# The MLP's gate row in four column tiles, sent through DRAM to all partitions, and the doubled columns of the norms on VectorE

## The chip, the cores and the metric

The kernel runs on one core of a Trainium2 chip. The metric is the device time of one execution in microseconds; the median of several runs is compared. A core has TensorE (PE; its weight loads are shown apart as PEld), VectorE (DVE), ScalarE (ACT), GpSimd (POOL) and SyncE (SP), which run side by side and wait for one another through semaphores. SyncE and GpSimd also issue most of the DMAs: SyncE's go to the queue that the profile calls q1, GpSimd's to q0. An engine takes its instructions in the order of the program, so an instruction that waits holds up everything behind it on that engine, DMA issues included.

## The reference

A transformer block on x of 2048 x 576, with a conditioning vector c. `mod` is a row of six vectors of 576: shift, scale and gate for the attention (sa, ca, ga) and for the MLP (sb, cb, gb).

```python
mod = (silu(c) @ w_mod).reshape(c.shape[0], 6, 1, -1)
sa, ca, ga, sb, cb, gb = ...
h = layernorm(x) * (1 + ca) + sa
x = x + ga * A(h, wqkv, wo)          # 32 heads of 18, each position sees 8 positions, 2 apart
h = layernorm(x) * (1 + cb) + sb
x = x + gb * (((h @ w_gate) * (h @ w_up)) @ w_down)     # 576 -> 4608 -> 576
return x
```

The change touches how gb is computed and spread, and one part of how layernorm's output is written.

## The kernel before

The 2048 rows are cut into eight chunks of 256, each of two tiles of 128 rows. The chunks form five groups for the MLP: [0], [1, 2], [3, 4], [5, 6], [7]. A setup stage (to about 48 us) computes the modulation, the whole attention of chunk 0 and parts of chunks 1 and 2. Then, for every group, `gate_up` computes gate, up and their product hh over 36 steps f of 128 hidden columns, and `down` multiplies hh with w_down. Between the steps of one group stand pieces of the attention of the next chunks, so that TensorE always has matmuls.

The order on every engine is that of the program text. The function `timed` decides it: it walks over the gate steps of a group, keeps a clock of TensorE (`t`) and one of VectorE, and places a waiting piece as soon as the marks that it needs are due. A piece is a tuple (TensorE time, VectorE time, needed marks, its mark, time until the mark, call). The numbers are estimates written by hand; a different estimate for one piece can move other pieces to another step. A gate step is a pair of half matmuls: `Pair.first` of the new step stands ahead of `Pair.second` of the one before.

D is 576, P is 128. 576 columns are four full tiles of 128 and a rest of 64, so the last tile of weights has only 64 rows. For the matmuls of pairs, which use the array as two halves of 64 rows, the last 64 columns of the normalized rows are written twice (columns 512 to 575 and again 576 to 639): the "doubled columns". `norm` (L280) does both writes on VectorE, `norm_act` (L287) does both on ScalarE, after a small VectorE instruction for the bias (L285). `norm_act` writes the doubled columns for chunk 3 ahead of the attention and for chunk 1 ahead of the MLP.

`mod_row` computes one row of 576 of the modulation already spread over all 128 partitions: `sc_bc` holds silu(c) in 128 equal columns, so each output partition gets the same row. That is two PSUM tiles (512 and 64 columns) with five matmuls each (L356) and two copies on ScalarE (L358, L359). It is used for ga (in the setup) and for gb: `gb_row`, which is a piece of group 0's `gate_up`. gb_bc, 128 x 576 in f32, is read for the first time at the end of group 0's `down`, where VectorE multiplies acc and accr with it (L949, L954, in the last group L996).

The weights of the gate row are loaded by `load_wm5` on GpSimd's queue: four row tiles into the free end of the hh tile, the last 64 rows into an output tile (wm5r, shown as o_t). Behind it on the same queue stand `load_wd(0)` and then, in `gb_row` after `mod_row`, `ld_d1(3)`: the load of block 3 of w_down, 576 KB, also into the free end of hh.

Weights of gate and up come in nine blocks per group (four steps each), gate and up as one load of 512 KB each, on SyncE's queue (L154). In group 0, blocks 0 to 2 are loaded in the setup, block 3 goes to the free end of hh, block 4 is asked for at step 4, block 5 at step 8, and so on. Step f uses block f // 4. On the same queue stand the transposes by DMA: of the normalized rows of chunk 3 into hT (L394), and of the attention's logits into lg_t (L487). The kernel starts its projections of chunk 3 (`qk_pair`, L706 with wqk) when hT has been modulated by VectorE (L302).

PSUM tiles are taken in turn from eight banks. Each DMA queue counts its DMAs on eight semaphores in turn, so that an issue also waits for the DMA eight places earlier.

Of the kernel before, what the change touches and what calls it, by code (L numbers as in the profile page):

```python
# [7 lines left out]
BF = mybir.dt.bfloat16  # L8
F32 = mybir.dt.float32
ALU = mybir.AluOpType  # L10
ACTF = mybir.ActivationFunctionType
# [7 lines left out]
P = 128  # L19
D = 576  # L20
DP = 640
KT = 5
KF = 4
H = 32
# [2 lines left out]
DIL = 2  # L27
FF = 4608
FT = FF // P
HALO = 16  # L30
SPAN = 14
EPS = 1e-5
# [12 lines left out]
def kernel(  # L45
# [13 lines left out]
    nc = tc.nc  # L59
# [9 lines left out]
    consts = pool("consts", 1)  # L69
    wts = pool("wts", 1)  # L70
    dramp = pool("dramp", 1, space=DRAM)
# [19 lines left out]
    def ps(shape, dt, name):  # L91
        return psp.tile(shape, dt, name=name, tag="bank")
# [8 lines left out]
    eps = consts.tile([P, 1], F32, name="eps")  # L101
    modc = consts.tile([P, 4, KT], F32, name="modc")
    ga_bc = consts.tile([P, D], F32, name="ga_bc")
    gb_bc = consts.tile([P, D], F32, name="gb_bc")
    sc_bc = consts.tile([P, KT, P], BF, name="sc_bc")
    xns = [consts.tile([P, ST, DP], BF, name=f"xn{k}") for k in range(2)]
    o_sb = consts.tile([P, ST, DP], BF, name="o_sb")
# [2 lines left out]
    qTs = [consts.tile([P, KT, CH], BF, name=f"qT{k}") for k in range(2)]  # L110
    kTs = [consts.tile([P, KT, HALO + CH], BF, name=f"kT{k}") for k in range(2)]
    oT = consts.tile([P, KT, CH], BF, name="oT")
    wv = wts.tile([P, KT, D], BF, name="wv")
    wo = wts.tile([P, KT, D], BF, name="wo")
    vd = dramp.tile([HALO + S, D], BF, name="vd")
    prod_t = consts.tile([P, 4 * KT * CH], BF, name="prod_t")
    prod_n = [0]

# [19 lines left out]
    def load_res(i):  # L138
        x_res[i] = xres.tile([P, ST, D], BF, name="x_r")
        nc.sync.dma_start(x_res[i][:], x_rows(i))  # L140

    wgu_blk, wgu_in, wd_blk, wd_home, wgu_home = {}, {}, {}, {}, {}
    NG = len(GROUPS)
    NBLK = FT // FB

# [17 lines left out]
    def load_wd(g):  # L163
        if g >= NG * NBLK:
            return
        r0 = (g % NBLK) * FB * P
        wb = wd_home.pop(g, None)
        if wb is None:
            wb = wdp.tile([P, FB, D], BF, name="wd")
        wd_blk[g] = wb  # L170
        return nc.gpsimd.dma_start(wb[:], B_w_down[r0:r0 + FB * P, :].rearrange("(k p) n -> p k n", p=P))  # L171
# [38 lines left out]
    for xn_t in xns:  # L210
# [12 lines left out]
                            pattern=[[-1, P + 2 * SPAN]], channel_multiplier=1)  # L223
    zrow = sp.tile([HALO, D], BF, name="zrow")
    nc.gpsimd.memset(zrow[:], 0.0)
    nc.gpsimd.dma_start(vd[0:HALO, :], zrow[:])
    nc.gpsimd.memset(wqk[64:, KF, :], 0.0)
    for k in range(2):
# [10 lines left out]
                            base=-DIL * (W - 1), pattern=[[DIL, W], [0, H]], channel_multiplier=1)  # L239
    edge = sp.tile([HALO, W - 1, P], BF, name="edge")  # L240
    edge_t = sp.tile([P, HALO], BF, name="edge_t")
    ash_e = sp.tile([P, H], BF, name="ash_e")
# [17 lines left out]
    def ln_parts(src, tag, act=False, both=None):  # L260
        stats = small.tile([P, ST, 2, 6], F32, name="ln_stats" + tag)
        mv = small.tile([P, ST, 2], F32, name="ln_mv" + tag)
        rstd = small.tile([P, ST], F32, name="ln_rstd" + tag)
        xn = xns[turn[0] % 2]
        turn[0] += 1
        both = tag == "b" if both is None else both

        def stat(j, hfs=(0, 1)):
            for hf in hfs:
                nc.vector.bn_stats(stats[:, j, hf, :], src(j)[:, hf * 288:(hf + 1) * 288])  # L270
            if hfs[-1] == 1:
                nc.vector.bn_aggr(mv[:, j, :], stats[:, j, :, :].rearrange("p a b -> p (a b)"))

        def rsq(r):
            nc.scalar.activation(rstd[:, r], mv[:, r, 1], ACTF.Ln, bias=eps[:])
            nc.scalar.activation(rstd[:, r], rstd[:, r], ACTF.Exp, scale=-0.5)

        def norm(j):
            for d0, s0, n in ((0, 0, D), (D, D - 64, 64))[0:2 if both else 1]:
                nc.vector.tensor_scalar(xn[:, j, d0:d0 + n], src(j)[:, s0:s0 + n], mv[:, j, 0:1], rstd[:, j:j + 1],  # L280
                                        ALU.subtract, ALU.mult)

        def norm_act(j):
            nb = small.tile([P, 1], F32, name="ln_nb")
            nc.vector.scalar_tensor_tensor(nb[:], mv[:, j, 0:1], -1.0, rstd[:, j:j + 1], ALU.mult, ALU.mult)  # L285
            for d0, s0, n in ((0, 0, D), (D, D - 64, 64))[0:2 if both else 1]:
                nc.scalar.activation(xn[:, j, d0:d0 + n], src(j)[:, s0:s0 + n], ACTF.Identity, bias=nb[:], scale=rstd[:, j:j + 1])  # L287
        return xn, stat, rsq, (norm, norm_act) if act is None else norm if not act else norm_act

    def layernorm(src, tag, act=False, both=None):  # L290
# [30 lines left out]
    def mod_columns(wm, pi, fill=lambda: None, steps={}):  # L321
        pm = ps([P, 320], F32, "pm")
        order = (KF, 0, 1, 2, 3)
        for kt in order:
            for q in range(4):
                rows = slice(0, P) if kt < KF else slice(64 * (q // 2), 64 * (q // 2) + 64)
                c0 = (q // 2) * D + (q % 2) * 256
                nc.tensor.matmul(pm[H * q:H * (q + 1), :], lhsT=sc_bc[rows, kt, 0:H], rhs=wm[rows, kt, c0:c0 + 320],
                                 start=(kt == order[0]), stop=(kt == order[-1]), skip_group_check=True)
            steps.get(kt, nop)()  # L330
        mrow = sp.tile([P, 320], BF, name="mrow")
        nc.scalar.copy(mrow[:], pm[:])
        fill()
        tr = ps([P, 3, P], BF, "pm_t")
        for n in range(2):
            nc.tensor.transpose(tr[:, n, :], mrow[:, n * P:(n + 1) * P], ident[:])
        for r in (slice(0, 64), slice(64, P)):
            nc.tensor.transpose(tr[r, 2, :], mrow[:, 2 * P:], ident[:])
        c01 = slice(2 * pi, 2 * pi + 2)

        def adds():
            nc.vector.tensor_tensor(modc[:, c01, 0:KF].rearrange("p b (u v) -> p b u v", v=2),
                                    tr[:, 0:2, :].rearrange("p v (b u x) -> p b u v x", b=2, u=2)[:, :, :, :, 0],
                                    addc[:, :, 0:KF].rearrange("p b (u v) -> p b u v", v=2), ALU.add)
            nc.vector.tensor_tensor(modc[:, c01, KF:KT], tr[:, 2, :].rearrange("p (b x) -> p b x", b=2)[:, :, H:H + 1],
                                    addc[:, :, KF:KT], ALU.add)
        return adds

    def mod_row(wm, dst):
        pa = ps([P, 512], F32, "pa")  # L350
        pb = ps([P, 64], F32, "pb")
        for p_t, c0, c1 in ((pa, 0, 512), (pb, 512, D)):
            for kt in range(KT):
                m = wm(kt)
                rows = slice(0, m.shape[0])
                nc.tensor.matmul(p_t[:], lhsT=sc_bc[rows, kt, :], rhs=m[:, c0:c1],  # L356
                                 start=(kt == 0), stop=(kt == KT - 1))
        nc.scalar.copy(dst[:, 0:512], pa[:])  # L358
        nc.scalar.copy(dst[:, 512:D], pb[:])  # L359


    scale = float(DH) ** -0.5
# [498 lines left out]
    def gate_items(gi):  # L861
        n = len(GROUPS[gi])
        own = 0.15 * n + 0.06
        if gi != 1:
            return [("f", f, 1.0 * n, own, "") for f in range(FT)]
        return [("f0", f, 1.04, 0.28, "") for f in range(HEAD)] + [("f1", f, 1.04, 0.28, "h2") for f in range(HEAD)] + [("f", f, 2.0, own, "") for f in range(HEAD, FT)]

# [43 lines left out]
    def down(gi, hh, bg):  # L911
        grp = GROUPS[gi]
        nj = ST * len(grp)
        last = FT - FB
        at, late = among(last, 0.25 * nj, bg)
# [3 lines left out]
        def mm_a(f, j):  # L919
            wb = wd_blk[gi * NBLK + f // FB]  # L920
            nc.tensor.matmul(acc[j][:], lhsT=hh[:, f, js(j)], rhs=wb[:, f % FB, 0:512],  # L921
                             start=(f == 0), stop=(f == FT - 1))

        def mm_r(f, j):
            wb = wd_blk[gi * NBLK + f // FB]
            nc.tensor.matmul(accr[:, j, :], lhsT=hh[:, f, js(j)], rhs=wb[:, f % FB, 512:D],  # L926
                             start=(f == 0 and j == 0), stop=(f == FT - 1), skip_group_check=True)

# [81 lines left out]
    wm5r = outp.tile([P, D], BF, name="o_t")  # L1010

    def wm5():
        return spare[0][:, 8 * NB:8 * NB + FB * D].rearrange("p (k d) -> p k d", d=D)

    def load_wm5():
        nc.gpsimd.dma_start(wm5(), w_mod[0:KF * P, 5 * D:6 * D].rearrange("(k p) n -> p k n", p=P))
        nc.gpsimd.dma_start(wm5r[0:64, :], w_mod[KF * P:D, 5 * D:6 * D])

# [236 lines left out]
        load_wd(k)  # L1255

    def gb_row():
        mod_row(lambda k: wm5()[:, k, :] if k < KF else wm5r[0:64, :], gb_bc)
        ld_d1(3)

    first = attention_of(1, 2)[12:-14]
# [6 lines left out]
    at = [k for k, p in enumerate(first) if p[3] == "o11"][0] + 2  # L1268
    first[at] = (0.6, 0, "o11", "-", 0, lambda: b_o(1))
    gbg = {0: (qkv_of(3, "p17 z3"),  # L1270
               [[(0, 0, "", "-", 0, lambda: (load_wm5(), load_wd(0))), (0, 0, "", "z3", 8.0, both_halves), (0, 0, "", "w5", 12.0, nop), (1.5, 0, "w5", "-", 0, gb_row), (0, 0, "", "-", 0, lambda: load_res(2))],
                first,
                norm_of(3, "", "", 5) + [(0, 2.5, "", "m4", 0.2, lambda: a_ln(4)), (0, 0, "m4", "r4", 1.0, lambda: aa[4]["rsq"]()),
                                         (0, 0, "r4", "e4", 2.0, lambda: aa[4]["norm"]((0,))), (0, 0, "e4", "n4", 1.6, lambda: aa[4]["norm"]((1,))),
# [37 lines left out]
    for gi, grp in enumerate(GROUPS):  # L1312
        hh_t = hhp.tile([P, FT * 2 * CH], BF, name="hh")
        n = CH * len(grp)
# [45 lines left out]
```

## Time and profile before

| | |
|---|---|
| runs | 543.72, 544.71, 546.10 us; median 544.71 |
| the profiled execution | 544.44 us |
| its span | 542.7 us |
| TensorE, VectorE, ScalarE, GpSimd busy | 535.3, 315.9, 251.5, 67.9 us |
| TensorE's granted clock | 1.0 over the whole span |
| L356, gate row: matmuls 128x512 and 128x64 | 5 of 0.38 us, 5 of 0.19 us, from 62.7 to 64.2 us |
| L358, L359: copies to gb_bc | 0.585 and 0.218 us, from 64.1 us |
| L287: 128x576 alone, and with the 128x64 behind it | 0.865, 1.20 us |
| L280: 128x64 on VectorE | 0.292 us |
| DMA moved, 48 to 60 us; 60 to 70; 70 to 80; 95 to 128 | 343, 319, 264, 242 GB/s |

The span runs from the first instruction to the last; the time of an execution is a little longer. Durations of matmuls overlap, since they are pipelined: what a group of them costs is read from where the next group starts. A number in brackets behind an instruction is how long its engine stood idle before it and what ended that. The DMA view gives, for a stretch of time, the packets and bytes of each queue and the time from an issue to its landing.

### The profile page before, as it was taken

The page shows a single profiled execution, that of the slowest core. Times are in us where ns is not written, and L with a number is a line of the kernel's source. Part 1 is how long each engine was busy: PE and PEld are TensorE (multiplying, and loading weights), DVE is VectorE, ACT ScalarE, POOL GpSimd, SP SyncE. Part 2 cuts the span into 40 slices and gives each one's busy share as a digit, 9 for nine tenths or more (in the row PEclk, how much of TensorE's full clock was granted, in tenths as well). Part 3 has the DMA queues.
Part 4 walks back from the last instruction along what each step waited for, and adds up shares of the span by engine and source line. Part 5 has one row for each costly group of instructions (what it writes and reads, how often), then busy time and mean ns, then how long its engine had stood idle before and what let it go on. Part 6 is the DMA issues. An engine that isn't in the chain of part 4 may idle for free.

```text
span 542.7 us, 14569 instructions
## 1 busy us (share of the span) xinstructions
PE 535.3 (99%) x6157; PEld 321.9 (59%) x6189; DVE 315.9 (58%) x713; ACT 251.5 (46%) x617; POOL 67.9 (13%) x104
## 2 busy tenths in 40 slices
PE   8999999999999999999999999999999999999997
PEld 4887789756745444555544444555544445558875
DVE  4989586777766777646358896524344924032212
ACT  4776777543566553022645552014555551006630
POOL 7104012122000110111000110110010101010210
PEclk9999999999999999999999999999999999999999
DMA  8999999778872694878435983894296592849821
GB/s 264 299 261 363 336 272 332 258 224 258 267 203 89 211 208 153 227 220 293 135 108 163 232 288 68 162 239 159 89 275 176 156 311 69 255 138 294 271 74 42
DMA packets 94924, 114.52 MB, mean 211 GB/s; under 512 B 27980, under 2 KB 83676, under 8 KB 94732
## 3 DMA queue, kind: packets, MB, share of 16 engines
q1 hardware_dynamic: 83360, 67.29, 44.6%
q0 software_dynamic: 11344, 46.25, 27.8%
q8 instruction: 48, 0.79, 0.6%
q14 instruction: 16, 0.13, 0.1%
q10 hardware_dynamic: 156, 0.07, 0.0%
HBM read 103.15 MB, written 4.74 MB: 199 GB/s over the span
## 4 chain that ended last, share of the span: by engine, by line
PE 94%; DMA 3%; DVE 1%; SPq 1%; ACT 1%; issue 0%
PE pg L706 28%; PE pu L706 23%; PE acc L921 19%; PE pq L706 3%; PE accr L926 3%; PE pw L605 3%; PE pq L416 3%; PE acc L976 3%; PE lgT L470 2%; DMA wmC<-in_w_mod_dram 2%; PE pv L706 2%; PE pv L439 1%; DMA wqk<-in_A_wqkv_dram 1%; PE po L567 1%; PE pwj L584 0%
## 5 line engine op out<-in xcount | busy, mean ns | idle before, releaser
L706 PE MATMUL pg<-h2T,wgu 64*128 64x512 bf16 (+1 forms) x1376 | 265.5, 331 | 0.0
L706 PE MATMUL pu<-h2T,wgu 64*128 64x512 bf16 (+1 forms) x1376 | 264.5, 331 | 0.0
L706 PEld LDWEIGHTS <-wgu 64*128 64x128 bf16 x2752 | 136.5, 94 | 94.8 <-issue 0.5
L757 ACT CAST u_sb<-pu 128x512 bf16<-128x512 f32 (+1 forms) x172 | 85.4, 497 | 135.8 <-PE pg L706 131.2
L760 DVE TENSOR_TENSOR hh<-g_sb,u_sb 128x512 bf16<-128x512 bf16 x136 | 57.4, 423 | 116.2 <-ACT g_sb L758 115.7
L758 ACT CAST g_sb<-pg 128x512 bf16<-128x512 f32 (+1 forms) x172 | 86.7, 504 | 0.0
L921 PEld LDWEIGHTS <-hh 128*128 128x128 bf16 x504 | 49.0, 98 | 59.5 <-issue 1.5
L921 PE MATMUL acc<-wd,hh 128*128 128x512 bf16 x329 | 84.1, 380 | 0.1
L926 PE MATMUL accr<-wd,hh 128*128 128x64 bf16 x344 | 62.4, 193 | 0.7
L706 PE MATMUL pu<-h2T,wgr 64*128 64x512 bf16 (+1 forms) x188 | 61.5, 327 | 0.2 <-ACT u_sb L757 0.2
L706 PE MATMUL pg<-h2T,wgr 64*128 64x512 bf16 (+1 forms) x188 | 61.5, 327 | 0.0
L926 PEld LDWEIGHTS <-hh 128*128 128x128 bf16 x504 | 45.8, 98 | 1.9
L171 POOL DMA_DIRECT2D wd<-in_B_w_down_dram x29 | 21.8, 752 | 190.0 <-PE accr L926 93.4
L461 DVE TENSOR_TENSOR prod_t<-qT,kT 128x1280 bf16<-128x1280 bf16 x56 | 43.7, 818 | 0.7 <-ACT kT L777 0.7
L514 DVE TENSOR_TENSOR vsh<-vsh,attn 128x1152 bf16<-128x1152 bf16 x56 | 39.6, 748 | 1.2 <-DMA vsh<-vd 1.2
L706 PEld LDWEIGHTS <-wgr 64*128 64x128 bf16 x376 | 19.7, 94 | 15.4 <-issue 2.5
L921 PE MATMUL acc<-prod_t,hh 128*128 128x512 bf16 x111 | 28.8, 380 | 0.0
L304 ACT ACTIVATE h2T<-h2T,modc 128x256 bf16<-128x256 bf16 x12 | 6.6, 595 | 45.3 <-DMA h2T<-xn 45.3
L455 POOL DMA_DIRECT2D vsh<-vd x14 | 12.5, 897 | 104.8 <-DVE o_sb L524 89.6
L706 PE MATMUL pq<-hT,wqk 64*128 64x256 bf16 (+1 forms) x360 | 22.2, 259 | 0.1
L416 PE MATMUL pq<-hT,wqk 128*128 128x256 bf16 (+1 forms) x225 | 21.2, 251 | 0.4 <-ACT hT L304 0.4
L926 PE MATMUL accr<-prod_t,hh 128*128 128x64 bf16 x112 | 21.6, 193 | 0.1
(208 smaller groups left out, 605.0 us busy)
## 6 DMA issues: line engine op xcount, KB each, us to landing
wgu<-in_B_w_gate_dram SPq DMA_DIRECT2D x41, 512.0 KB, 4.5
wgu<-in_B_w_up_dram SPq DMA_DIRECT2D x41, 512.0 KB, 6.4
wd<-in_B_w_down_dram POOLq DMA_DIRECT2D x29, 576.0 KB, 5.6
vsh<-vd POOLq DMA_DIRECT2D x14, 1152.0 KB, 9.3
prod_t<-in_B_w_down_dram POOLq DMA_DIRECT2D x8, 576.0 KB, 7.6
hh<-in_B_w_down_dram POOLq DMA_DIRECT2D x6, 576.0 KB, 6.4
x_r<-in_A_x_dram SPq DMA_DIRECT2D x8, 288.0 KB, 8.3
vd<-v_sb POOLq DMA_DIRECT2D x16, 144.0 KB, 5.2
```

The lines of the kernel that those rows point to most:

```text
L171: return nc.gpsimd.dma_start(wb[:], B_w_down[r0:r0 + FB * P, :].rearrange("(k p) n -> p k n", p=P))
L416: nc.tensor.matmul(pq[:, gi, :], lhsT=wqk[:, kt, m * P:(m + 1) * P], rhs=hT[:, kt, cols], start=(kt == order[0] and not (by_k and gi)), st ...
L461: nc.vector.tensor_tensor(prod, aa[i]["qT"][:], aa[i]["kT"][:, :, off:off + CH], ALU.mult)
L514: nc.vector.tensor_tensor(v, v, at, ALU.mult)
L605: nc.tensor.matmul(pw[:], lhsT=oT[:, m, js(j)], rhs=wo[:, m, 0:512], start=(m == 0), stop=(m == KT - 1))
L706: return nc.tensor.matmul(out, lhsT=lhs, rhs=rhs, start=first, stop=last, skip_group_check=True)
L757: nc.scalar.copy(u[:, c, :], pu)
L758: nc.scalar.copy(g[:, c, :], pg)
L760: return lambda: nc.vector.tensor_tensor(hh[:, f - c:f + 1, :], g, u, ALU.mult)
L921: nc.tensor.matmul(acc[j][:], lhsT=hh[:, f, js(j)], rhs=wb[:, f % FB, 0:512], start=(f == 0), stop=(f == FT - 1))
L926: nc.tensor.matmul(accr[:, j, :], lhsT=hh[:, f, js(j)], rhs=wb[:, f % FB, 512:D], start=(f == 0 and j == 0), stop=(f == FT - 1), skip_grou ...
L976: nc.tensor.matmul(acc[i][:], lhsT=hh[:, f, js(j)], rhs=wb(f)[:, c0:c1], start=(f == 0), stop=(f == FT - 1))
```

## The change

Three things are changed.

1. The gate row is computed by a new function, `gb_cols`. The 576 columns are cut into four parts of 144 (GC). Part q goes to PSUM partitions 32q to 32q + 31: 20 matmuls of 32 weight columns by 144, in one PSUM tile. One copy brings it to `grow` (128 x 144, bf16). A DMA writes partitions 0, 32, 64 and 96 of it to a DRAM tile `gd` of 4 x 144, and a second DMA reads the 576 numbers from there into every partition of gb_bc. Both are issued by GpSimd. gb_bc is now bf16. The last row tile of the weights is used with all 128 rows, so rows 64 to 127 of wm5r are first set to zero by GpSimd.
2. `norm_act` writes only the 576 columns on ScalarE; the doubled columns come from a VectorE instruction as in `norm`.
3. The planner's TensorE time for the gate row is 0.85 instead of 1.5.

```diff
+GC = D // 4
-    gb_bc = consts.tile([P, D], F32, name="gb_bc")
+    gb_bc = consts.tile([P, D], BF, name="gb_bc")
+    grow = consts.tile([P, GC], BF, name="grow")
+    gd = dramp.tile([4, GC], BF, name="gd")
...
         def norm_act(j):
             nb = small.tile([P, 1], F32, name="ln_nb")
             nc.vector.scalar_tensor_tensor(nb[:], mv[:, j, 0:1], -1.0, rstd[:, j:j + 1], ALU.mult, ALU.mult)
-            for d0, s0, n in ((0, 0, D), (D, D - 64, 64))[0:2 if both else 1]:
-                nc.scalar.activation(xn[:, j, d0:d0 + n], src(j)[:, s0:s0 + n], ACTF.Identity, bias=nb[:], scale=rstd[:, j:j + 1])
+            nc.scalar.activation(xn[:, j, 0:D], src(j)[:, 0:D], ACTF.Identity, bias=nb[:], scale=rstd[:, j:j + 1])
+            if both:
+                nc.vector.tensor_scalar(xn[:, j, D:], src(j)[:, D - 64:D], mv[:, j, 0:1], rstd[:, j:j + 1], ALU.subtract, ALU.mult)
...
+    def gb_cols(wm):
+        pa = ps([P, GC], F32, "pa")
+        for kt in range(KT):
+            for q in range(4):
+                nc.tensor.matmul(pa[H * q:H * (q + 1), :], lhsT=sc_bc[:, kt, 0:H], rhs=wm(kt)[:, GC * q:GC * (q + 1)],
+                                 start=(kt == 0), stop=(kt == KT - 1), skip_group_check=True)
+        nc.scalar.copy(grow[:], pa[:])
+        nc.gpsimd.dma_start(gd[:], grow[0:P:H, :])
+        nc.gpsimd.dma_start(gb_bc[:], bass.AP(gd.tensor, gd.offset, [[0, P], [1, D]]))
...
     def load_wm5():
+        nc.gpsimd.memset(wm5r[64:, :], 0.0)
         nc.gpsimd.dma_start(wm5(), w_mod[0:KF * P, 5 * D:6 * D].rearrange("(k p) n -> p k n", p=P))
         nc.gpsimd.dma_start(wm5r[0:64, :], w_mod[KF * P:D, 5 * D:6 * D])
...
     def gb_row():
-        mod_row(lambda k: wm5()[:, k, :] if k < KF else wm5r[0:64, :], gb_bc)
+        gb_cols(lambda k: wm5()[:, k, :] if k < KF else wm5r[:])
         ld_d1(3)
...
-(1.5, 0, "w5", "-", 0, gb_row)
+(0.85, 0, "w5", "-", 0, gb_row)
```

In the order of the instructions this moves, apart from what is added and removed: one gate pair of group 0 (the first half of step 20 and the second half of step 19) from behind the first projection of chunk 3 to ahead of it, with its copies and its multiply; one multiply of the attention of chunk 1 by one place; and on SyncE's queue the second lg_t transpose of chunk 2 from ahead of the two loads of block 7 to behind them. On GpSimd's queue the two new DMAs stand behind `load_wd(0)` and ahead of `ld_d1(3)`.

More of the change, by code (lines that the diff above doesn't have):

```diff
@@ L1270 @@
     gbg = {0: (qkv_of(3, "p17 z3"),
-               [[(0, 0, "", "-", 0, lambda: (load_wm5(), load_wd(0))), (0, 0, "", "z3", 8.0, both_halves), (0, 0, "", "w5", 12.0, nop), (1.5, 0, "w5", "-", 0, gb_row), (0, 0, "", "-", 0, lambda: load_res(2))],
+               [[(0, 0, "", "-", 0, lambda: (load_wm5(), load_wd(0))), (0, 0, "", "z3", 8.0, both_halves), (0, 0, "", "w5", 12.0, nop), (0.85, 0, "w5", "-", 0, gb_row), (0, 0, "", "-", 0, lambda: load_res(2))],
                 first,
```

## The prediction

> **What bounds the kernel now.** I read the page first, then the timeline around the gate row, then the DMA view in short windows, then the timeline at the first projection of chunk 3. The page's head says who is the bound:
>
> ```profile
> span 542.7 us, 14569 instructions
> PE 535.3 (99%) x6157; PEld 321.9 (59%) x6189; DVE 315.9 (58%) x713; ACT 251.5 (46%) x617; POOL 67.9 (13%) x104
> ```
>
> TensorE is busy for 99% of the span, so a microsecond that it no longer spends is a microsecond of the end, unless a wait takes it back. Around the gate row (timeline; start, duration, engine, line, and in brackets the idle time before and what ended it):
>
> ```profile
> 58.91 0.85 PEld L706 LDWEIGHTS <-wgu 64*128 64x128 bf16 x16 [0.46 <-issue]
> 60.95 0.45 PEld L470 LDWEIGHTS <-ind 128*32 128x32 bf16 x20 [0.21 <-DVE mx L494]
> 61.61 0.10 PEld L706 LDWEIGHTS <-wgr 64*128 64x128 bf16 x2 [0.21 <-DVE dd L495]
> ...
> 62.70 0.55 PEld L356 LDWEIGHTS <-sc_bc 128*128 128x128 bf16 x4 [0.21 <-issue]
> 64.22 0.10 PEld L706 LDWEIGHTS <-wgr 64*128 64x128 bf16 x2
> 64.61 0.37 SPq L154 DMA_DIRECT2D wgu<-in_B_w_up_dram  x1
> 64.63 0.33 PEld L706 LDWEIGHTS <-hh 64*128 64x128 bf16 x7 [0.28 <-DMA hh<-in_B_w_up_dram]
> ```
>
> See three things. The gate row holds TensorE from 62.70 to 64.22, 1.52 us. Right behind it TensorE stands 0.28 us for weight block 3, which lands only then; SyncE's next load starts in the same moment (the waits of its queue name the same landing, 3.6 us). And at 58.91 there is a stall whose chain of waits leads through ScalarE:
>
> ```profile
> 57.40 1.20 ACT L287 ACTIVATE xn<-x_t,ln_nb,ln_rstda 128x576 bf16<-128x576 bf16 x2
> 58.51 0.34 ACT L757 CAST u_sb<-pu 128x256 bf16<-128x256 f32 x1
> ```
>
> The DMA view says why block 3, asked for at 41.7, takes 22.9 us. First 52 to 56 us, then 64 to 65 us (packets, MB, share of 16 engines):
>
> ```profile
> q0 software_dynamic: 268, 1.16, 85.1%
> q1 hardware_dynamic: 254, 0.21, 18.4%
> ```
> ```profile
> q1 hardware_dynamic: 298, 0.30, 106.7%
> q0 software_dynamic: 4, 0.01, 3.2%
> ```
>
> While GpSimd's queue (q0) has work, SyncE's (q1) gets 0.05 MB/us; once q0 is empty, 0.30 to 0.35. So here q0's loads decide when block 3 and all behind it land.
>
> **The change, part by part.**
> *Gate row on TensorE.* Ten matmuls (five 128x512, five 128x64) become 20 of 32 columns by 144. The nearest row is lgT (L470): 20 of 32 columns by 256 hold TensorE from 60.95 to 61.61, 0.66 us with the switch back. If four run side by side and the stream sets the pace, five rounds less 112 columns each take 5 x 112/256 of 0.53 us (five rounds of the 0.107 us step seen between matmuls of 256) = 0.23 less: 0.43. If issue sets it, lgj (L1076), 20 of only 32 streamed columns, shows 0.49 on the chain of waits, and with the 0.21 of the switch 0.70. I take 0.55: saved 1.52 - 0.55 = 0.97 (bounds 0.82 and 1.09). The Trainium skill (TensorEngine Tiling (Array Packing), Instruction Overhead) gives each matmul about 60 cycles whatever its size; an estimate from that page, with a cycle taken as 0.107 us / 256, is 20 x 25 ns = 0.50 us and with the switch 0.71. By it the saving would be 0.81 instead of 0.97.
>
> *Copies on ScalarE.* 0.58 + 0.22 us become one of 128x144, about 0.3 (between 0.26 for 64x128 and 0.42 for 128x320). ScalarE waits 0.37 us right after, so nothing follows.
>
> *Doubled columns.* Four ScalarE instructions go; the two for chunk 3 (here) cost 1.20 - 0.865 (one 128x576 alone) = 0.34 us in the first pair, and that pair holds the copies that TensorE waits for: 0.34 of the 0.46 stall is saved. The second pair ends at 60.76 with no stall behind it: 0. VectorE gets four of 0.292 us (L280, 128x64). The first delays its hh multiply, of which 1.11 us of idle before 59.70 is the cover; without it, 0.29. The two of chunk 1 lie in the first down pass, where TensorE shows no wait for them: 0, between -0.3 and +0.3.
>
> *gb_bc in bf16.* The multiplies with acc take 692 ns (128x512, f32 source). L495, with bf16 inputs and only its output f32, takes 692 too, an all-bf16 multiply (L760) 423. One f32 side is enough for the slow form, and acc stays f32: 0. The other bound is 0.27 in each of three changes of group and in the tail: -1.1.
>
> *Memset on GpSimd.* 0.57 (L230), in an idle gap of 0.45 before the load of the gate weights: they go out 0.15 to 0.2 later. They land at 61.0, wanted at 62.4: covered; uncovered 0.2.
>
> *What the two DMAs push back.* GpSimd's queue is in order, and behind them stands the load of wd block 3 (0.59 MB), which in the timeline of before goes out at once:
>
> ```profile
> 52.07 0.80 POOL L171 DMA_DIRECT2D wd<-in_B_w_down_dram  x1
> 52.86 0.76 POOL L171 DMA_DIRECT2D hh<-in_B_w_down_dram  x1
> 79.17 0.75 POOL L171 DMA_DIRECT2D wd<-in_B_w_down_dram  x1 [25.55 <-DMA lg_t<-lgs]
> ```
>
> The second line will wait for the row's copy (63.4) and then for gd's landing: 2.1 us (vd store at 112.7, light load) to 6.0 (vd store at 18.4, q1 full), so it goes out between 66 and 70. It is used after 98, so it is not late itself. Two effects follow. First, q0 from 52 us on carries 3.21 - 0.59 = 2.62 MB and is empty at about 61.2 instead of 64; by then q1 has moved 0.48 of the 1.01 MB it moves up to 64.6, and the other 0.53 at 0.33 MB/us is done at 62.8. Block 3 lands 1.7 us earlier, and TensorE, which comes 0.97 + 0.34 earlier (64.35 - 1.31 = 63.04), doesn't wait: 0.28 more. Together **1.59 us at 63**. Second, at 67 to 71 q0 gets 0.59 + 0.15 (gb_bc, 128 rows of 1,152 B) = 0.74 MB, 2.64 us at 0.28 MB/us, in which q1 loses 85% of its rate: 2.24 us.
>
> *What is late next.* q1 then carries weight block 5 and the transposes of hT for chunk 3. They landed like this:
>
> ```profile
> 72.33 1.37 DVE L302 TENSOR_SCALAR hT<-hT,modc 128x256 bf16<-128x256 bf16 x5 [1.40 <-DMA hT<-xn]
> 73.14 0.45 PEld L706 LDWEIGHTS <-wqk 64*128 64x128 bf16 x9 [0.21 <-DVE hT L302]
> ```
>
> hT came at 72.3, and the first projection followed VectorE closely. Now 72.3 - 1.7 + 2.24 = 72.8. The planner, told 0.85 instead of 1.5 for the gate row, puts one gate pair (its first half and the second of the pair before, 0.87 us, ending at 74.73 before) ahead of this projection, so that work is done by then; it needs block 5, which landed at 70.9 and now at 71.4, wanted at 71.55. The projection ends 1.37 + 0.15 us after hT lands: 72.8 + 1.52 = 74.3, against 74.73 for the same work before. **Kept: 0.4 us.** Block 4, landed at 68.07 and wanted at 68.36, moves with block 3. SyncE's second lg_t transpose goes behind block 7's two loads, some 2 us; its reader is VectorE at 92.2: covered. Blocks 6 to 8 are wanted 1.6 us and more after they land.
>
> *Sum.* The profiled execution took 544.44 us, span 542.7 and 1.74 around it; the median of the three runs is 544.71, 0.27 above. 542.7 - 0.4 = 542.3; on the median's footing **544.3 us**.
>
> **Rivals.**
> *The gain is kept.* If gd lands late (6 us and the 10.8 us that the v_e load took, for gb_bc ahead of it), wd block 3 moves after hT is in: 1.59 us stay, 543.1. For it: those two rows. Against: 0.74 MB anywhere ahead of 71 catches hT. The Trainium skill (DMA: Bandwidth & Descriptors, the anatomy of one DMA) has a fixed cost of about 2.0 us for a DMA on this path; by that estimate gd is in at 65.5, gb_bc behind it moves at once, and this rival falls.
> *Slower: the moved load with no relief before it.* If the transposes of hT go out at 65.1 as before, because what SyncE waits for there isn't freed by an emptier q0, hT lands at 72.3 + 2.24 = 74.5, the projection ends at 76.0 instead of 74.7: 546.0. It decides from a first transpose later than about 64.5. Against it: the queue's wait is named as block 3's landing.
> *The multiplies get faster* with bf16: 0.4 + 1.1, 543.2; with the gain kept as well, 542.0. Against it: L495.
> *The column tiles don't overlap:* 20 x 0.06 (144 columns) + 0.21 = 1.4, and the row saves 0.1; TensorE reaches hT's landing late enough not to wait there, and 0.0 to 0.5 is left: 544.5.
>
> **How the numbers follow.** Forecast 0.42, gain kept 0.27, slower 0.17, faster multiplies 0.06, no overlap 0.08. Predicted is the first, 544.3. The range goes down to 542.5 (kept gain, 543.1, less part of the multiplies' bound and 0.3 for chunk 1) and up to 546.1 (the slower rival). 0.5%, about what a measurement of this kernel can tell from no change, is 2.7 us: below 542.0 or above 547.4. Only the multiplies' bound with all gain kept reaches the one side (0.06), only a slower rival with further waits behind it the other (0.08).
>
> **What would show it.** Right: gate-row matmuls over some 0.5 us of TensorE; no wait for block 3 and its landing near 62.8; GpSimd's issue of wd block 3 after 66; q1's share down to a fifth while it moves; hT for chunk 3 near 72.8; o_t multiplies still 692 ns. Wrong: first transposes of hT not before 65, hT before 71.5, new waits of TensorE for weight blocks 4 or 5, or any stage after 100 us that takes longer than before.

## The result, and the profile after

The changed kernel takes 546.46 us (median of 22 runs, 545.09 to 548.03), the kernel before 543.92 (22 runs, 543.54 to 546.10). The ratio is 1.0041, with a 95% interval of 1.0032 to 1.0051: 0.4% slower, just outside the range of the forecast. The forecast stood on a median of three runs, 544.71; so -0.4 us was forecast as a change, and about +2.2 us came of it. (Ratios here are those of the comparison of the runs, not the quotient of two medians.) The profiled execution of the changed kernel took 546.59 us, with a span of 544.9. From the page (head, row of the engines, chain of waits by engine and by line):

```profile
span 544.9 us, 14624 instructions
PE 536.4 (98%) x6199; PEld 321.6 (59%) x6199; DVE 318.0 (58%) x717; ACT 249.7 (46%) x612; POOL 69.7 (13%) x107
PE 90%; DMA 6%; DVE 2%; SPq 0%; issue 0%; ACT 0%
PE pg L720 28%; PE pu L720 23%; PE acc L935 20%; PE pw L619 3%; PE pq L720 3%; PE accr L940 3%; PE acc L990 3%; DMA v_e<-vd 2%; PE pq L430 2%; DMA wgu<-in_B_w_up_dram 2%; PE lgT L484 2%; PE pv L720 2%; DMA vd<-v_sb 1%; DMA wmA<-in_w_mod_dram 1%; PE pv L453 1%; DVE prod_t L475 1%
```

In the chain of before, DMA has 3% and TensorE 94%; now it is 6% and 90%. New in its list are four DMAs, above all the load of v_e in the setup and a weight block of the gate steps (2% each); wmC and wqk are gone from it. The span is 2.2 us longer although the gate row itself got shorter. The timeline of the changed kernel shows the places of the prediction (start, duration, engine, line, operation, and in brackets the idle time before and what ended it):

```profile
50.89 0.10 PEld L720 LDWEIGHTS <-wgr 64*128 64x128 bf16 x2
...
59.46 0.87 ACT L289 ACTIVATE xn<-x_t,ln_nb,ln_rstda 128x576 bf16<-128x576 bf16 x1
60.23 0.35 ACT L771 CAST u_sb<-pu 128x256 bf16<-128x256 f32 x1
...
64.43 0.31 PEld L357 LDWEIGHTS <-sc_bc 128*32 128x32 bf16 x20 [0.21 <-issue]
64.86 0.10 PEld L720 LDWEIGHTS <-wgr 64*128 64x128 bf16 x2
64.87 0.45 PEld L720 LDWEIGHTS <-hh 64*128 64x128 bf16 x8
...
65.72 0.61 POOL L360 DMA_DIRECT2D gd<-grow  x1 [10.68 <-ACT grow L359]
72.36 0.57 POOL L361 DMA_DIRECT2D gb_bc<-gd  x1 [6.04 <-DMA gd<-grow]
72.93 0.78 POOL L174 DMA_DIRECT2D hh<-in_B_w_down_dram  x1
73.07 1.52 DVE L306 TENSOR_SCALAR hT<-hT,modc 128x256 bf16<-128x256 bf16 x5 [1.49 <-DMA hT<-xn]
...
81.06 0.09 PEld L720 LDWEIGHTS <-wqk 64*128 64x128 bf16 x1 [1.10 <-issue]
83.30 0.33 PEld L720 LDWEIGHTS <-wgu 64*128 64x128 bf16 x7 [0.98 <-DMA wgu<-in_B_w_up_dram]
...
100.29 0.10 PEld L935 LDWEIGHTS <-hh 128*128 128x128 bf16 x1 [0.21 <-issue]
```

The lines of the kernel before that answer to the first gate step, the wait at 81 us and the start of the down pass:

```profile
48.83 0.10 PEld L706 LDWEIGHTS <-wgr 64*128 64x128 bf16 x2
...
81.03 0.42 PEld L706 LDWEIGHTS <-wqk 64*128 64x128 bf16 x8 [0.33 <-issue]
...
98.11 0.10 PEld L921 LDWEIGHTS <-hh 128*128 128x128 bf16 x1 [0.21 <-issue]
```

The gate row holds TensorE from 64.43 to 64.86, 0.43 us where it held it 1.52, and weight block 3 (hh) follows with no wait. On ScalarE the pair of 1.20 us is one instruction of 0.87. So far the change does what it says. But all of this starts late: the first gate step begins at 50.89, against 48.83 before. That is 2.06 us lost in the setup, where no instruction was changed. From there the two timelines can be laid side by side: the changed kernel is 2.06 us behind at the first gate step, 1.74 at lgT (62.69 against 60.95, the ScalarE stall is gone), 0.64 behind the gate row (64.86 against 64.22), 0.36 behind block 3, whose wait is gone. Then it loses 0.77 more at 81.06 (a wait of 1.10, 0.33 before, for ScalarE's copies of qT; ScalarE itself has waited 1.42 us for VectorE there) and 0.98 at 83.30 for weight block 6: together 2.11. The down pass of group 0 starts 2.18 us late (100.29 against 98.11), and after it every stage takes as long as before: 423.1 us from there to the last down pass in both. That stretch is 423.1 us in the trace of every variant below that computes the block, so all that is lost or won is decided ahead of it.

The 2.06 us of the setup come through two DMAs on the chain of waits of the changed kernel:

```profile
18.84 6.47 DMA vd<-v_sb
25.59 12.04 DMA v_e<-vd
38.02 0.16 DVE modc L346
```

The DMA view of the same stretch, 20 to 48 us, shows that the whole core moved less; first the kernel before, then the changed one:

```profile
DMA packets 6025, 8.64 MB, mean 308 GB/s; under 512 B 374, under 2 KB 5127, under 8 KB 5892
```
```profile
DMA packets 5571, 7.83 MB, mean 280 GB/s; under 512 B 371, under 2 KB 4766, under 8 KB 5438
```

The transfers of this stretch run at 280 GB/s instead of 308. No instruction of the change lies ahead of 48 us. What it does change for the setup is where the tiles lie: gb_bc shrinks from 2,304 to 1,152 B per partition and grow adds 288, so every tile allocated behind them moves down by 864 B. By the allocation of the two programs, the tiles of the weights lie at multiples of 64 B before (wgu at 142,272, wd at 166,848, hh at 191,936, each 64 B beside a multiple of 128) and 32 B beside multiples of 64 after. For v_e, the tile of the load that became slower, it is the other way round: 32 B beside a multiple of 64 before (214,048), on one after.

### The profile page after: what moved, and what is told of

Its sections match the earlier page's. It is cut to its first block, busy times and chain, and to the rows that moved or that the text cites. A ratio compares the mean times of both kernels' runs of the same rounds, so it can differ in the third digit from the quotient of the medians.

```text
span 544.9 us, 14624 instructions
## 1 busy us (share of the span) xinstructions
PE 536.4 (98%) x6199; PEld 321.6 (59%) x6199; DVE 318.0 (58%) x717; ACT 249.7 (46%) x612; POOL 69.7 (13%) x107
## 4 chain that ended last, share of the span: by engine, by line
PE 90%; DMA 6%; DVE 2%; SPq 0%; issue 0%; ACT 0%
PE pg L720 28%; PE pu L720 23%; PE acc L935 20%; PE pw L619 3%; PE pq L720 3%; PE accr L940 3%; PE acc L990 3%; DMA v_e<-vd 2%; PE pq L430 2%; DMA wgu<-in_B_w_up_dram 2%; PE lgT L484 2%; PE pv L720 2%; DMA vd<-v_sb 1%; DMA wmA<-in_w_mod_dram 1%; PE pv L453 1%; DVE prod_t L475 1%
## 5 line engine op out<-in xcount | busy, mean ns | idle before, releaser
L935 PE MATMUL acc<-wd,hh 128*128 128x512 bf16 x344 | 86.0, 381 | 0.0
```

## The experiments

**1. Is it the addresses, or the moved load?** Four kernels. The first is the change with 864 B put back, so that all later tiles lie where they lay; the second is the kernel before with 32 B put in.

```diff
 e1_after_pad, the changed kernel:
     grow = consts.tile([P, GC], BF, name="grow")
+    pad = consts.tile([P, 432], BF, name="pad")
 e2_before_shift, the kernel before:
     gb_bc = consts.tile([P, D], F32, name="gb_bc")
+    pad = consts.tile([P, 16], BF, name="pad")
 e3_after_d1_first, the changed kernel:
     def gb_row():
         gb_cols(lambda k: wm5()[:, k, :] if k < KF else wm5r[:])
-        ld_d1(3)
...
-(0, 0, "", "-", 0, lambda: (load_wm5(), load_wd(0)))
+(0, 0, "", "-", 0, lambda: (load_wm5(), load_wd(0), ld_d1(3)))
 e4_after_pad_d1: e1 and e3 together
```

> The changed kernel with an unused tile of 864 bytes behind grow, so that every tile after it lies at the address that it had before. Theory S (the smaller gb_bc moves all later tiles by 864 bytes, from multiples of 64 to 32 beside them, and that slows the setup by about 2 us; the moved load of wd block 3 costs about 1.8 later; the gate row and the norms win 1.6): about +0.2 us against the kernel before, first gate step near 48.8 us as before. Theory L (addresses do nothing, the profiled setup was an odd execution, and the moved load costs more than is won): about +2.2 us, like the changed kernel.

> The kernel before with an unused tile of 32 bytes behind gb_bc, so that every later tile lies 32 bytes beside a multiple of 64; nothing else differs. Theory S: about +2.0 us, first gate step near 50.8 instead of 48.8 us. Theory L: 0.0 (within 0.3), first gate step near 48.8.

> The changed kernel with the load of wd block 3 issued ahead of the two new DMAs, right behind wd block 0, as before. Theory S: the setup's 2 us stay and the 1.8 of the moved load go, so about +0.4 us. Theory L: the moved load is the whole loss, so -1.0 to -1.6 us.

> The changed kernel with both: the old addresses and the load of wd block 3 in its old place. Theory S: -1.0 to -1.6 us against the kernel before. Theory L: the same as e3, -1.0 to -1.6.

| kernel | median, us | ratio to before, 95% |
|---|---|---|
| e1, change at the old addresses | 544.39 (before: 543.73) | 1.0002, 0.9991 to 1.0013 |
| e2, before + 32 B | 546.57 | 1.0044, 1.0028 to 1.0060 |
| e3, change, wd block 3 ahead of the two DMAs | 546.10 | 1.0043, 1.0028 to 1.0058 |
| e4, e1 with wd block 3 ahead | 544.77 | 1.0013, 1.0000 to 1.0027 |

The kernel before becomes as slow as the changed one by 32 unused bytes alone, and the change at the old addresses shows no difference from before. The setup follows (DMA view, 20 to 48 us; first e1, then e2):

```profile
DMA packets 6370, 8.65 MB, mean 309 GB/s; under 512 B 389, under 2 KB 5564, under 8 KB 6237
```
```profile
DMA packets 5765, 8.04 MB, mean 287 GB/s; under 512 B 379, under 2 KB 4960, under 8 KB 5632
```

Their first gate steps start at 48.59 and 50.12 us. The setup is only half of what e2's trace loses. Its down pass starts 2.65 us late (100.76): 1.29 us come from the setup, 0.93 from a longer wait for weight block 3 (0.28 in the trace of before), 0.43 from further on.

```profile
66.85 0.33 PEld L707 LDWEIGHTS <-hh 64*128 64x128 bf16 x7 [1.21 <-DMA hh<-in_B_w_up_dram]
```

A late first gate step alone does not make the loss: in e7 (below) it starts at 50.12 too, and the down pass only 0.61 us late (98.72); in e17 it starts at 49.69 and the down pass 0.17 late (98.28). The place of the load of wd block 3, the concern of the forecast, is not the loss: put ahead of the two new DMAs, as it stood before, it brings nothing at the new addresses (1.0043 against 1.0041) and nothing at the old ones (1.0013 against 1.0002, overlapping). One thing doesn't fit neatly: in e3's profile the setup is quick (310 GB/s, first gate step at 49.02), and that execution, 544.81 us, is the fastest of its 12. So the slow setup is not in every execution, or not alone; where a typical execution of e3 loses its time was not profiled.

**2. Which addresses?** The kernel before moved by other amounts, and the change moved by 832 instead of 864 B, which leaves its tiles on multiples of 64.

```diff
 e7_before_shift64, e16_before_shift128, e17_before_shift512, the kernel before, n = 32, 64, 256:
     gb_bc = consts.tile([P, D], F32, name="gb_bc")
+    pad = consts.tile([P, n], BF, name="pad")
 e10_after_pad32, the changed kernel:
     grow = consts.tile([P, GC], BF, name="grow")
+    pad = consts.tile([P, 16], BF, name="pad")
```

> The kernel before with an unused tile of 64 bytes behind gb_bc: all later tiles move, but stay at multiples of 64. If it is the place beside a multiple of 64 that costs: 0.0 (within 0.3 us). If any move of the addresses costs: about +2 us, like e2.

> The changed kernel with an unused tile of 32 bytes behind grow: all later tiles lie 832 bytes below their old addresses, at multiples of 64 again. Theory 64 (only the place relative to 64 bytes counts): like e1, 0.0 against the kernel before, within 0.5 us. Theory A (the exact addresses count): between 0.5 and 2.3 us slower.

> The kernel before with all later tiles moved by 128 bytes, so that they keep their place relative to 128 (64 beside a multiple). Theory C (a class of addresses decides: before, e1 and e6 at 64 beside a multiple of 128 show 0.00 to 0.02%, e7 and e10 at multiples of 128 0.11 and 0.18%, e2, e3 and the changed kernel at 32 beside a multiple of 64 0.41 to 0.44%): 0.0, within 0.3 us. Theory A (each address has its own time): 0.5 us or more to either side.

> The kernel before with all later tiles moved by 512 bytes: the place relative to 64, 128, 256 and 512 is kept. Theory C: 0.0, within 0.3 us. If this moves as much as e7 or e10, those 0.1 to 0.2% are what any build of this kernel can differ by, and no class below 64 can be told.

| moved by | kernel | median, us | its before | ratio, 95% |
|---|---|---|---|---|
| +512 B | e17 | 543.83 | 543.85 | 1.0000, 0.9990 to 1.0009 |
| +64 B | e7 | 545.01 | 544.07 | 1.0011, 0.9998 to 1.0024 |
| +128 B | e16 | 544.83 | 543.85 | 1.0013, 1.0003 to 1.0024 |
| -832 B | e10 | 544.82 | 544.05 | 1.0018, 1.0006 to 1.0030 |
| -864 B | the change | 546.46 | 543.92 | 1.0041, 1.0032 to 1.0051 |
| +32 B | e2 | 546.57 | 543.73 | 1.0044, 1.0028 to 1.0060 |

The kernels whose weight tiles lie 32 B beside a multiple of 64 lose 0.4% (e3, at the addresses of the change, does too), and the others lose 0 to 0.2%; the intervals of e10 and e2 just touch. Within the others the simple rules fall: "only multiples of 64 count" would make e7, e10 and e16 equal to before, "the place modulo 128 counts" would do so for e16. Both e10 and e16 have an interval that lies wholly above 1, if only just; e7's reaches below it. Only the moves of 0 and 512 B show no cost at all. Whether a period (256 or 512 B) is behind that was not tried.

**3. The loads by themselves.** A kernel that holds only loads of the shapes of the weights and computes nothing: 36 times two loads of 512 KB on SyncE's queue into wgu tiles, and with every second of them one of 576 KB on GpSimd's queue into a wd tile. Then the same with the tiles moved.

```diff
 e8_dma_aligned, and again e14_dma_aligned_again: tiles at multiples of 128
 e9_dma_shifted (n = 16), e13_dma_shift64 and again e15_dma_shift64_again (n = 32):
+    pad = consts.tile([P, n], BF, name="pad")      ahead of all tiles
 e11_dma_q0_shifted: 32 B between the wgu and the wd tiles (only GpSimd's targets move)
 e12_dma_q1_shifted: 32 B ahead of the wgu tiles and 32 B ahead of the wd tiles (SyncE's move by 32, GpSimd's by 64)
```

> Only loads, nothing of the reference is computed and the output is zero: 72 loads of 512 KB of w_gate and w_up on SyncE's queue and 18 of 576 KB of w_down on GpSimd's, the forms of group 0, into four buffers each, tiles at multiples of 64 bytes. It gives the time that the loads take alone. Theory S: 2 to 8% shorter than e9.

> e8 with every tile 32 bytes beside a multiple of 64. Theory S (writes into such tiles are slower): 2 to 8% longer than e8 (the setup moved 8% less per time), some 3 to 11 us. Theory T (the loads themselves are as fast, and the engines are what suffers): the same time within 0.5%.

> e8 (loads only, output zero) with only the tiles of w_down, loaded on GpSimd's queue, 32 bytes beside a multiple of 64; those of w_gate and w_up stay at multiples. e8 moved 380 GB/s against e9's 355 only in the first 40 us, while GpSimd's queue had loads, and 348 in both after it. If GpSimd's loads are what suffers: like e9, 2 to 3 us longer than e8. If SyncE's are: like e8.

> e8 with only the tiles of w_gate and w_up, loaded on SyncE's queue, 32 bytes beside a multiple of 64. If GpSimd's loads are what suffers: like e8 (within 0.3 us). If SyncE's are: 2 to 3 us longer.

> e8 with all tiles moved by 64 bytes. Theory 64: like e8, within 0.3 us. If any move costs: 1 to 3 us longer.

> e8 once more, the same kernel (loads only, output zero), now beside e15 on one chip. If its shorter time belongs to its addresses: 148 us and 380 GB/s again while both queues load. If it was that one chip or load: 150.7 us and 355 GB/s.

> e13 once more beside e14. If the addresses decide: 150.7 us, 2.5 above e14. If not: the same as e14 within 0.5 us.

| | median, us | GB/s from 5 to 35 us |
|---|---|---|
| e8, e14: multiples of 128 | 148.16, 148.67 | 381 (e8) |
| e9: all moved by 32 | 150.83 | 355 |
| e11: GpSimd's targets by 32 | 150.62 | 356 |
| e12: SyncE's by 32, GpSimd's by 64 | 151.03 | 355 |
| e13, e15: all by 64 | 150.68, 150.87 | 355 (e13) |

Each has two to four runs. The pages' rows of the DMA's rate in 40 slices, e8 first, then e9, show where the loss lies:

```profile
GB/s 102 373 384 379 382 383 380 385 383 383 380 358 347 348 349 348 348 348 349 349 347 349 349 348 347 349 349 348 348 351 349 347 348 349 349 347 349 359 371 162
```
```profile
GB/s 111 370 355 354 354 358 351 355 353 356 356 347 348 348 348 348 348 348 348 348 349 348 348 348 348 348 348 348 348 349 350 348 348 348 348 348 348 356 372 173
```

GpSimd's queue has loads in the first eleven slices only. From the third slice to the eleventh the rate is 379 to 385 GB/s in e8 and 351 to 358 in e9; behind them, with SyncE's queue alone, it is about 348 in both. So the address of a load's target costs 7% of the DMA rate while both queues load, and nothing while SyncE's loads alone. Moving GpSimd's targets alone (e11) gives the full loss. SyncE's targets were never moved alone: e12 moves GpSimd's by 64 B as well, and e13 shows that a move of all by 64 B gives the full loss too, so whether SyncE's matter stays open.

The rule of these loads is not the rule of the kernel. In the kernel before, wgu, wd and hh lie 64 B beside a multiple of 128, as wgu and wd do in e13, where the loads are slow; in e7 and e10 they lie on multiples of 128, as in e8, where the loads are fast, and neither is faster than the kernel before. So the loads show that a target's address can cost DMA rate. That the tiles of the weights are what costs the kernel 0.4% is not shown; which of its many tiles do it, and how, is open.

**4. Where the gain of the change goes.** At the old addresses (e1) the gate row, the norms and block 3 are all quicker, and the end is the same. The timeline of e1 near the end of group 0's gate steps:

```profile
91.33 0.10 PEld L721 LDWEIGHTS <-wgr 64*128 64x128 bf16 x2
91.35 0.10 PEld L721 LDWEIGHTS <-wgu 64*128 64x128 bf16 x1
92.96 0.77 PEld L721 LDWEIGHTS <-wgu 64*128 64x128 bf16 x15 [1.52 <-DMA wgu<-in_B_w_up_dram]
```

TensorE arrives 2.5 us ahead of before at step 24 (79.33 against 81.81), and 1.5 us ahead at the last weight block, 8 (91.33 against 92.84; of the 2.5 us about 1.0 is the new order, which puts a gate pair ahead of a projection), but that block lands only at 92.9. Its load of w_up went out at 80.14, 2.5 us earlier than before (82.62, landed 91.2), and took 12.8 us instead of 8.6, because three loads of w_down went out on GpSimd's queue at 79.19, 79.94 and 80.68, about when they did before (79.17 to 80.64). The DMA view from 86 to 92.5 us, before first, then e1 (packets, MB, share of 16 engines):

```profile
q1 hardware_dynamic: 1830, 1.85, 89.8%
q0 software_dynamic: 41, 0.11, 5.0%
```
```profile
q1 hardware_dynamic: 1153, 1.16, 54.8%
q0 software_dynamic: 277, 1.13, 49.9%
```

Before, the three loads are nearly done at 86 us and SyncE's queue has the engines; in e1 they still move 1.13 MB, half of the engines' time. So I held these loads back until block 8 is in, in e1 and in the kernel before, and then took away the planner's new time as well:

```diff
 e5_after_pad_late (e1) and e6_before_late (the kernel before):
-(0, 20): lambda: behind(load_wd(1), wgu_in[6]), (0, 21): lambda: ld_d1(4), (0, 22): lambda: load_wd(2)
+(0, 25): lambda: behind(load_wd(1), wgu_in[8]), (0, 26): lambda: ld_d1(4), (0, 27): lambda: load_wd(2)
 e18_after_pad_late_plan (e5):
-(0.85, 0, "w5", "-", 0, gb_row)
+(1.5, 0, "w5", "-", 0, gb_row)
```

> e1 (the changed kernel at the old addresses) with the three loads of w_down that go out at 79 us (wd blocks 1, 4 and 2) held back until weight block 8 of gate and up has landed. Theory D (the won TensorE time comes back as the wait for weight block 8, because the queues share one bandwidth and 1.77 MB of w_down run beside it): block 8 lands before 90 us instead of 92.9, no wait for it, and 1.0 to 1.6 us are won against the kernel before. Theory W (the win is lost elsewhere, or w_down then comes late for the down pass): 0 or slower, a wait for wd after 98 us.

> The kernel before with the same three loads held back. Theory D: block 8 wasn't waited for in the kernel before, so 0.0 (within 0.4). If this gains as much as e5, the gain of e5 is not the change's.

> e5 (the changed kernel at the old addresses, three loads of w_down held back until weight block 8 has landed) with the planner's time of the gate row back at 1.5, so that the order of all other pieces is that of the kernel before. Theory D (with the bandwidth out of the way the won TensorE time stays, 1.09 for the gate row and 0.35 for the norms): 1.0 to 1.6 us faster than the kernel before, at least as much as e5. If the planner's new order is worth something of its own: less than e5 by 0.3 us or more.

| kernel | median, us | its before | ratio, 95% |
|---|---|---|---|
| e5 | 543.62 | 544.07 | 0.9987, 0.9974 to 0.9999 |
| e6 | 543.92 | 544.07 | 1.0001, 0.9988 to 1.0014 |
| e18 | 542.96 | 544.08 | 0.9983, 0.9973 to 0.9993 |

In e5 the wait is gone; the lines that answer to those of e1:

```profile
91.14 0.10 PEld L721 LDWEIGHTS <-wgr 64*128 64x128 bf16 x2
91.16 0.86 PEld L721 LDWEIGHTS <-wgu 64*128 64x128 bf16 x16
```

Block 8 landed at 86.2, the down pass starts at 96.42 instead of 98.09, and the span is 541.0, 1.7 us below before's and 1.1 below e6's (542.1). The hold-back alone (e6) is worth nothing: before, TensorE comes late enough for block 8 anyway. So the gain was there and was taken by the next transfer in line. That rests on the traces: the intervals of e1 and e5 overlap. e18 shows that the planner's new time, 0.85, has no part in the gain: with the old order the time is not higher. Whether the old order would have kept the gain without the hold-back was not tried. e18 is the fastest of all versions that ran, 0.17% below before; over its 12 runs the gain is about 0.9 us (0.0017 of 544.08), less than its profile's 1.7.

## Why the prediction was off

*The step that failed* is the one on **gb_bc in bf16**. It asked only what the narrower type does to the multiplies, and there it was right: 692 ns before and after, since acc is f32.

```profile
L968 DVE TENSOR_TENSOR o_t<-acc,gb_bc x14: 690/692/692, 130.1 to 488.0; 128x512 bf16<-128x512 f32 x14
```

(operation, count, least, median and largest ns, first and last start.) What it priced at 0 was the edit, and the edit also frees 864 B ahead of nearly every other tile. That term is +0.4%, 2.2 us by the ratio (0.0041 of 543.92), and it is the whole difference within the noise: with the bytes put back, e1 is 1.0002, and 32 B put into the kernel before bring the same loss (e2, 1.0044). Why an address costs the kernel that much stays open. The forecast said that the stages up to 48 us are untouched, by listing no term there; the profile has 2.06 us there.

*The gate row*: 0.97 us saved by the forecast, 1.09 measured. The lower of its two estimates held: four tiles run side by side and the streamed columns set the pace; the row takes 0.43 us, 0.23 less than lgT with its 256 columns. The row behind the higher estimate, lgj, was no fit: its matmuls load weights of 128 columns, not of 32. The Trainium skill (TensorEngine Tiling (Array Packing), Instruction Overhead) gives each matmul about 60 cycles; by the estimate from it the row would hold TensorE 0.50 us, or 0.71 with the switch, and the trace has 0.43. Those cycles didn't add up over the four column tiles.

*Norms*: 0.34 forecast, 0.32 to 0.34 found, as 0.87 instead of 1.20 us on ScalarE and no stall of 0.46. *Block 3*: the wait of 0.28 is gone in both, as forecast; it landed at 60.4 in e1 (62.8 forecast). But the wait is missing in e6's trace too, where block 3 landed at 61.9, and up to 79 us e6 is the kernel before. So the 0.28 stands in one execution of the kernel before and not in the other, and the forecast had no ground to count it as a gain of the change. The memset took 0.57 us as forecast, and no wait followed.

*The two DMAs*: the row's copy landed in gd 5.8 us (e1) and 6.0 us (the change) after GpSimd began to wait, the upper of the two rows that the forecast had. The Trainium skill (DMA: Bandwidth & Descriptors, the anatomy of one DMA) has a fixed cost of about 2.0 us for a DMA on this path; the trace, with SyncE's queue at work on all engines (119% of them from 66 to 72 us, GpSimd's 0.3%), has about three times that. So the load of wd block 3 went out at 70.4 in e1, not before hT: hT came at 70.4, where 72.8 was forecast. The give-back at hT did not happen. Up to there the rival "the gain is kept" was right, in mechanism and in its reason.

*What took it back instead* is the sentence that blocks 6 to 8 are wanted 1.6 us and more after they land. That slack was read from the trace of before and left as it stood, although the same forecast moves both ends of it: TensorE comes earlier, and the load goes out earlier, into three loads of w_down that do not move. In e1 the slack of 1.6 us became a wait of 1.52. Thus the forecast of 0.4 us kept is within e1's interval (-0.5 to +0.7 us by its ratio), but that is luck: the gain was given back in another place. In group 0's gate steps the transfers come barely ahead of TensorE, and several variants wait for one weight block or another there (block 4, 1.08 us in e3; block 3, 0.91 in e4; block 6 in the change).

*The other rivals*: the multiplies got no faster, the column tiles do overlap, and hT was not late by itself: its time in the change, 73.07, is 0.74 behind before's, less than the 2.06 us by which the setup was late. The slower rival (546.0) came near the measured time by another mechanism, which doesn't count for it.

## What to carry to other kernels

A change of a tile's size or type moves all tiles allocated behind it: compare the addresses of the tiles that transfers fill, and where they change, test the old kernel with the same shift alone (a few unused bytes) before reading anything into the time. Where TensorE is gained ahead of a stage that is fed by transfers, follow every later load with both its moved issue and its moved use, up to the end of the stage; a slack read from the old trace is not a slack of the new one. And when a gain vanishes, look for the next wait and move what shares the bandwidth with it: here that turned 1.0002 (e1) into 0.9987 (e5), and 0.9983 with the old order (e18).

## What the runs showed of the hardware

The DMA rate depended on the address of the target in SBUF: with two queues loading, 381 GB/s at multiples of 128 B, and 355 to 356 with the targets of GpSimd's queue or of both moved by 32 or 64 B; with SyncE's queue alone, 348 in all cases. In the whole kernel a move of the tiles by 32 B cost 0.44%, and one by 512 B nothing; no one rule for the place of the weights' tiles fits both findings.

Twenty matmuls of 32 columns by 144 in four column tiles held TensorE for 0.43 us, behind an idle time of 0.21. A store of four rows, 1,152 B, took 6 us to land while SyncE's queue kept the engines full (119% of them from 66 to 72 us).
